# Memory denominators on GpSimd, a split last tile, four output buffers, an earlier load of x and a new order of work

## The chip, the cores and the metric

The kernel runs on one core of a Trainium2 chip. The time is device microseconds (us) for one execution of the whole program. The engines are TensorE (PE: matrix products), VectorE (DVE), ScalarE (ACT), GpSimd (POOL) and SyncE (SP, which here only issues transfers). They run side by side; each takes its own instructions strictly in the order in which the program lists them, and waits where one of them needs something that another engine or a transfer has not finished.

## What is computed

Two branches share one input x (2048 tokens, 512 features) and are mixed per token: `out = g * a + (1 - g) * b` with `g = sigmoid(x . gate_w)`.

Branch a is attention with a memory: 32 heads of 16 features, the tokens cut into 4 segments of 512. In each segment every head does causal softmax attention inside the segment, and reads a memory that the earlier segments have filled:

```python
p = softmax(q k^T * scale + mask);  a_dot = p v
pq = phi(q);  num = pq M;  den = pq z + 1e-06;  a_mem = num / den
o = sigmoid(beta) * a_mem + (1 - sigmoid(beta)) * a_dot
M = M + phi(k)^T v;  z = z + sum(phi(k))       # phi(t) = t + 1 for t > 0, else exp(t)
```

The outputs of the heads are multiplied by `wo`. Branch b is a gated feed-forward layer: `(gelu(x w_gate) * (x w_up)) w_down`, with 1792 hidden features. All tensors are bfloat16.

## The kernel before

**Tiling.** x is held transposed (`xT`: features on the 128 partitions, four chunks of features, 2048 tokens). A projection of 128 features for one segment is four matmuls of 512 columns; once the first logits have been made each is split into four column tiles that run at once (`mm4`). The pieces have short names with segment and index: `q`, `k`, `v` (projections), `gt` (two tiles of the gate projection), `up` (one tile), `lg` (a slot of logits of four heads, 20 slots a segment, numbered 0 to 79), `pv` (probabilities times values, for the even `e` or odd `o` heads of a chunk), `M` (memory update), `den` and `num` (memory denominators and numerators), `dn` and `wo` (one step of the down projection and of the output projection of 128 tokens, into the same accumulator).

**What follows each on other engines.** An `e` in front of a name is the evacuation of a PSUM result to SBUF (`eup2.9`, `epv0.3e`, `enum1.0`, `eden1`), by DVE or ACT. ACT does the exponentials of the logits (`ex20a`, `ex20b`) and the gelus (`egt`). GpSimd then zeroes the part of the exp tiles above the diagonal (`as20a`, `as20b`). `E`, `Q`, `Em`, `ph` make phi, the last on GpSimd. `ko` makes a copy of k for the odd heads. `r`, `rg`, `n`, `m`, `o` normalise the output of a chunk of eight heads, add the memory's part and transpose it into `xT`, where `wo` reads it. For the memory, `mbd` and `zbd` (DVE) lay M and z out by blocks; `eden` transposes the denominators, `rma` (`f_a`) spreads them over the partitions while adding 1e-06, `rmr` takes the reciprocal, `rmg` multiplies by the gate; then `nm` scales each `num`. `rma` is sixteen instructions of 32 partitions and 32 elements. `wos` scales `wo` once by the share of the direct attention. `os` scales a finished tile of 128 tokens into an output buffer `osb`, and `st` stores it.

**Buffers.** PSUM has two banks for most pieces (`gen`, a and b) and three double banks for logits and gate pairs (`lg`, a to c). A piece of TensorE cannot start before its bank's last content has been evacuated. In SBUF, rings of fixed size do the same (`RINGS`): twelve exp tiles `pT`, two `T` tiles of `pv`, one `rm`, one `Tm` (shared by `eden` and `enum`), two output buffers `osb`.

**The order is written out by hand.** `ORDER` lists every piece once; `Sched.run` emits them in that sequence, each to its engine. `#a` names the PSUM bank; `@A`, `@D`, `@P` choose ACT, DVE or POOL where a piece may run on several. So the order in the list is, engine by engine, the order in which each engine's queue is worked off.

**Loads.** All on SP's queue, in this order: the first half of `wk` and x of segment 0 (with ACT's queue), `wq`, the first 512 columns of `w_gate`, `wv`, the rest of `w_gate`, `w_up`, `gate_w`, `beta`, x of segments 1 to 3 (four transposing transfers each, `load_x`), `wo`. Then the transfers of `ORDER` follow (`pk`: transposing phi(k), `wdn`: the down weights, `st`: the stores).

**Around the change.** Between the logits of two segments (before `lg20`, `lg40`) TensorE does the seven gate pairs of a later segment, while ACT changes from exp to gelu and back; `den1` and `den2` fall there, and `den3` near `lg70`. In front of `lg0` it does the gate pairs of segments 0 and 1.

Of the kernel before, what the change touches and what calls it, by code (L numbers as in the profile page):

```python
# [49 lines left out]
lg16#ca ev1.1@D as14a v1.0#b ex16a up1.7#a ev1.0@D ex16b lg17#bc eup1.7 k1.2#b ex17a Emk1.0 r0.1  # L50
phk1.0 pv0.2o#a ek1.2@A lg18#ab ex17b epv0.2o v1.2#b ex18a k1.3#a ev1.2@D Eq1.0 lg19#ca ek1.3@D
q1.2#b ex18b r0.2 Emq1.0 up1.8#a Qq1.0 omz ex19a phq1.0 gt2.0#b eup1.8 o0.0 as17b M0.0#a rg0.1
Ek1.1 gt2.2#c pk1.0 as18a n0.1 eq1.2@A ex19b rg0.2 eM0.0 Emk1.1 up1.9#b eb egt2.0 as19b M0.1#a
gt2.3#a o0.1 Qk1.1 eM0.1 phk1.1 q1.3#a egt2.2 gt2.4#b eq1.3@A as18b Eq1.1 as15b as16b up1.13#a
as16a gt2.5#c as17a eup1.13 egt2.3 Qq1.1 zbd0 eup1.9 up1.10#a Emq1.1 n0.2 phq1.1 up1.11#b eup1.10
egt2.5 gt2.1#a eup1.11 mbd0 as19a den1#a egt2.1 gt2.6#c eden1 egt2.4 rma1 pv0.3e#b egt2.6 v1.3#a
epv0.3e lg20#ab ev1.3@D pv0.3o#b ex20a up1.12#a epv0.3o up2.0#b eup1.12 num1.0#a ex20b eup2.0
lg21#ca enum1.0 up2.1#b ex21a rmr1 up2.2#a ex21b as21a eup2.1 lg22#bc eup2.2 k2.0#b as21b ex22a
rmg1 k2.1#a nm1.0@P ek2.0@D ex22b lg23#ab ek2.1@D as20b num1.1#b ex23a as22a enum1.1 up2.3#a as22b
r0.3 ex23b as20a lg24#ca rg0.3 q2.0#b as23a eup2.3 ex24a nm1.1@P pv1.0e#a eq2.0@D Ek2.0 lg25#bc  # L60
ko1.2@P epv1.0e num1.2#b as24a ex24b enum1.2 up2.4#a as23b n0.3 ex25a as24b q2.1#b eup2.4 ex25b
lg26#ab nm1.2@D dn0.0.0#a Emk2.0 dn0.0.1 ex26a dn0.0.2 eq2.1@D dn0.0.3 dn0.0.4 ko1.1@D dn0.0.5
num1.3#b o0.3 ex26b lg27#ca dn0.0.6 enum1.3 dn0.0.7 ex27a dn0.0.8 as26b o0.2 dn0.0.9 dn0.0.10
pv1.0o#b wos ex27b as27a lg28#bc dn0.0.11 dn0.0.12 epv1.0o ex28a dn0.0.13 wo0.0.0 as26a wo0.0.1
wo0.0.2 wo0.0.3 ex28b as27b lg29#ab os0.0@D up2.6#b as25b ex29a as28a st0.0 as25a up2.5#a pk1.1
eup2.6 ex29b as29a lg30#ca eup2.5 pv1.1e#b ex30a as29b v2.0#a epv1.1e as28b ex30b r1.0 lg31#bc
ev2.0@D pv1.1o#b ex31a Qk2.0 v2.2#a ko1.3@D phk2.0 epv1.1o ex31b lg32#ab ev2.2@D v2.3#b rg1.0
ex32a dn0.1.0#a dn0.1.1 as31a ev2.3@D dn0.1.2 ex32b lg33#ca dn0.1.3 as30a n1.0 up2.7#b ex33a
dn0.1.4 eup2.7 dn0.1.5 ex33b dn0.1.6 lg34#bc m1.0@D v2.1#b ex34a as33b as32a dn0.1.7 ev2.1@D
dn0.1.8 dn0.1.9 ex34b ko2.0@P lg35#ab up2.8#b as30b ex35a as31b dn0.1.10 as32b eup2.8 dn0.1.11  # L70
dn0.1.12 lg36#ca as34b pv1.2e#b ex36a as35a dn0.1.13 as34a epv1.2e wo0.1.0 wo0.1.1 ex36b wo0.1.2
wo0.1.3 dn0.2.0#b dn0.2.1 dn0.2.2 os0.1@A dn0.2.3 lg37#ca st0.1 M1.0#a ex37a dn0.2.4 eM1.0 dn0.2.5
dn0.2.6 dn0.2.7 k2.2#a as37a as33a dn0.2.8 ek2.2@A dn0.2.9 dn0.2.10 dn0.2.11 ex37b dn0.2.12
dn0.2.13 pv1.2o#a Eq2.0 wo0.2.0 epv1.2o wo0.2.1 wo0.2.2 wo0.2.3 ex35b lg38#ca os0.2@D q2.2#a ex38a
Qq2.0 st0.2 dn0.3.0#b pk2.0 eq2.2@D dn0.3.1 dn0.3.2 dn0.3.3 r1.2 dn0.3.4 Emq2.0 dn0.3.5 dn0.3.6
r1.1 dn0.3.7 phq2.0 dn0.3.8 rg1.1 dn0.3.9 k2.3#a lg39#bc dn0.3.10 ex39a as36a dn0.3.11 ek2.3@D
dn0.3.12 dn0.3.13 ko2.1@P wo0.3.0 q2.3#a ex39b as37b wo0.3.1 as38a Ek2.1 eq2.3@D gt3.0#b as39a
as35b ex38b Qk2.1 Emk2.1 wo0.3.2 n1.1 phk2.1 egt3.0 gt3.4#c rg1.2 up2.10#a as36b Eq2.1 wo0.3.3
eup2.10 gt3.3#a as39b m1.1@D nm1.3@P os0.3@D M1.1#a gt3.1#b st0.3 egt3.3 eM1.1 as38b zbd1 mbd1
Qq2.1 pv1.3e#b Emq2.1 pv1.3o#a phq2.1 egt3.1 gt3.2#a epv1.3o egt3.4 o1.1 o1.0 gt3.5#b epv1.3e n1.2  # L80
r1.3 den2#a egt3.5 gt3.6#c eden2 egt3.2 rma2 up2.9#b egt3.6 lg40#ba eup2.9 up2.11#a ex40a up2.12#b
eup2.11 up3.0#a eup2.12 ex40b lg41#cb eup3.0 num2.0#b ex41a enum2.0 k3.0#a rmr2 up2.13#b ek3.0@A
rg1.3 rmg2 ex41b lg42#ac nm2.0@P eup2.13 up3.1#a ex42a n1.3 as41a up3.2#b eup3.1 ex42b lg43#ba
as40b eup3.2 num2.1#a as42a ex43a enum2.1 up3.3#b m1.2@D ex43b lg44#cb nm2.1@P eup3.3 k3.1#a ex44a
m1.3@D as43b q3.0#b ek3.1@D ex44b as42b lg45#ac eq3.0@D as40a num2.2#a ex45a as43a enum2.2 up3.4#b
# [934 lines left out]
```

## Time and profile before

| | us |
|---|---|
| median of 3 runs (lowest, highest) | 279.96 (279.3, 280.32) |
| profiled execution, whole | 279.55 |
| its span | 277.8 |
| TensorE busy | 266.5 (96%) |
| ACT busy | 218.4 (79%) |
| DVE busy | 178.2 (64%) |
| POOL busy | 151.6 (55%) |

The span runs from the first to the last instruction of the profiled execution. In the profile, PE is TensorE, PEld its weight loads, and SPq the queue of transfers that SP issues. L349 and the like are lines of the kernel; many pieces share the line of a helper, so they are told apart by the tile that they write (`dn`, `up`, `pv`). In a timeline a row is: start, duration, engine, line, operation, output<-input, shape, count; in square brackets stands how long the engine was idle ahead of it, and what it waited for. In a row of waits: who waited, for whom, us in total, times, longest. In a row of groups: busy us and mean ns behind the first bar, idle us behind the second. "PE busy" counts a matmul from its start to its modelled end, and they overlap.

### The profile page before, as it was taken

To read this page: it belongs to the slowest core of one execution; us is meant where nothing else is said; L and a number is where in the kernel's file an instruction comes from. 1 tells how busy PE (TensorE), PEld (TensorE's weight loads), DVE (VectorE), ACT (ScalarE), POOL (GpSimd) and SP (SyncE) were. 2 spreads that over 40 slices of the span, in tenths; PEclk is the share of its full clock that TensorE was granted. 3 is DMA by queue.
4 is the path that set the end of the run, shared out by engine and by line. 5 is a ranking of instruction groups with operands and counts; after the bars stand their busy time and mean duration, and the time that the engine had idled before them with its cause. 6 is when DMAs were issued, how large, how long until landed. Compare 5 with 4: busy or idle time off the path is not lost.

```text
span 277.8 us, 10843 instructions
## 1 busy us (share of the span) xinstructions
PE 266.5 (96%) x4855; PEld 129.0 (46%) x4855; DVE 178.2 (64%) x360; ACT 218.4 (79%) x234; POOL 151.6 (55%) x241
## 2 busy tenths in 40 slices
PE   7999999999999979999999998999999999899993
PEld 4644444444445544444454563444454454344541
DVE  1600026965878698997527688975947877956661
ACT  2388599999998985989875968989999898868400
POOL 8040004778846713954935940597597857349710
PEclk9999999999999999999999999999999999999999
DMA  6998492100002000003004000000002000100002
GB/s 207 371 286 107 95 310 67 33 12 2 4 2 42 2 0 2 2 2 59 2 24 61 2 21 2 2 2 22 2 5 59 2 22 2 40 22 21 21 2 79
DMA packets 22103, 14.07 MB, mean 51 GB/s; under 512 B 14120, under 2 KB 21032, under 8 KB 22056
## 3 DMA queue, kind: packets, MB, share of 16 engines
q1 hardware_dynamic: 21480, 12.85, 18.8%
q8 instruction: 38, 0.62, 1.0%
...
q14 instruction: 9, 0.07, 0.1%
HBM read 8.13 MB, written 2.10 MB: 37 GB/s over the span
## 4 chain that ended last, share of the span: by engine, by line
PE 78%; DVE 13%; DMA 6%; issue 1%; SPq 1%; ACT 0%; DVEq 0%; ACTq 0%
PE dn L349 19%; PE up L349 17%; PE lg L625 8%; PE gt L345 8%; PE gt L349 6%; PE pv L676 6%; PE v L349 4%; PE q L349 4%; DMA wga<-in_B_w_gate_dram 4%; PE k L349 4%; DVE rm L855 3%; DVE G L548 2%; DVE Mbd L816 1%; DMA out_dram<-osb 1%; DMA wdn<-in_A_x_dram 1%
## 5 line engine op out<-in xcount | busy, mean ns | idle before, releaser
L648 ACT ACTIVATE pT<-lg 128x1024 bf16<-128x1024 f32 x160 | 154.0, 1026 | 19.3 <-PE lg L625 18.1
L657 POOL TENSOR_SCALAR_AFFINE_SELECT pT<-pT 128x512 bf16<-128x512 bf16 (+1 forms) x160 | 88.5, 581 | 71.3 <-ACT pT L648 70.3
L349 PE MATMUL dn<-wdn,G 128*32 128x512 bf16 x896 | 59.3, 380 | 0.3 <-DVE T L694 0.3
L349 PE MATMUL up<-xT,wup 128*32 128x512 bf16 x896 | 56.1, 380 | 1.7 <-DVE G L548 1.2
L548 DVE TENSOR_TENSOR G<-up,G 128x512 bf16<-128x512 f32 x56 | 38.3, 688 | 19.0 <-PE up L349 15.5
L539 ACT ACTIVATE G<-gt 128x1024 bf16<-128x1024 f32 x28 | 27.4, 1022 | 9.3 <-PE gt L345 5.1
L349 PEld LDWEIGHTS <-wup 128*32 128x32 bf16 x896 | 23.3, 96 | 23.6 <-issue 5.8
L694 DVE STREAM_TRANSPOSE T<-pv 128x512 f32<-128x512 f32 x32 | 22.7, 710 | 17.5 <-PE pv L676 17.4
L349 PEld LDWEIGHTS <-G 128*32 128x32 bf16 x896 | 22.7, 96 | 21.5 <-issue 3.3
L211 DVE CAST vz<-v 128x512 bf16<-128x512 f32 x15 | 10.3, 689 | 28.9 <-PE v L345 25.3
L349 PE MATMUL gt<-xT,wga 128*32 128x512 bf16 x448 | 26.6, 379 | 0.0
L676 PE MATMUL pv<-pT,vz 128*32 128x256 bf16 (+2 forms) x640 | 23.1, 273 | 3.0 <-DVE T L694 1.7
L345 PE MATMUL gt<-xT,wga 128*128 128x512 bf16 x112 | 25.0, 379 | 0.1
L676 PEld LDWEIGHTS <-vz 128*32 128x32 bf16 x640 | 15.1, 97 | 12.4 <-issue 2.8
L751 POOL TENSOR_TENSOR pkT<-E,Q 128x1024 bf16<-128x1024 bf16 x6 | 12.8, 2128 | 13.4 <-DVE Q L744 6.4
L349 PE MATMUL dn<-wo,xT 128*32 128x512 bf16 x256 | 19.1, 380 | 0.0
L751 POOL TENSOR_TENSOR pq<-E,Q 128x1024 bf16<-128x1024 bf16 x6 | 13.2, 2194 | 10.6 <-DVE E L747 8.2
L349 PEld LDWEIGHTS <-wga 128*32 128x32 bf16 x448 | 12.9, 97 | 10.0
L625 PE MATMUL lg<-qT,kT 16*128 16x256 bf16 (+2 forms) x320 | 17.3, 274 | 0.0
L625 PE MATMUL lg<-qT,kO 32*128 32x128 bf16 (+2 forms) x320 | 17.3, 272 | 0.0
L345 PEld LDWEIGHTS <-wga 128*128 128x128 bf16 x112 | 10.8, 98 | 13.4 <-DMA wga<-in_B_w_gate_dram 0.6
L349 PEld LDWEIGHTS <-xT 128*32 128x32 bf16 x480 | 11.8, 96 | 11.0 <-issue 2.2
...
## 6 DMA issues: line engine op xcount, KB each, us to landing
...
wup<-in_B_w_up_dram SPq DMA_DIRECT2D x1, 1792.0 KB, 14.6
wdn<-in_B_w_down_dram SPq DMA_DIRECT2D x1, 1792.0 KB
...
```

Source lines behind the costliest of these rows:

```text
L211: nc.vector.tensor_copy(dst, src)
L345: nc.tensor.matmul(out, lhsT=lhsT, rhs=rhs, start=start, stop=stop)
L349: nc.tensor.matmul(out[a], lhsT=lhsT[:, a], rhs=rhs, start=start, stop=stop, tile_position=(0, 32 * j), skip_group_check=True)
L539: nc.scalar.activation(G[s][:, 2 * hp:2 * hp + 2, :], t[:, :, :], AF.Gelu_apprx_tanh)
L548: UPT[(s, hs)] = evac("DVE", g, box, lambda e, t: nc.vector.tensor_mul(G[s][:, hs, :], t[:, :], G[s][:, hs, :]), kind="up")
L625: nc.tensor.matmul(A[j // 2][:, j % 2, at * P:(at + nq) * P], lhsT=l, rhs=r, start=True, stop=True, tile_position=(32 * j, 0))
L648: nc.scalar.activation(pT[(s, t, h)][:, :, :], A[h][:, :, :], AF.Exp, scale=0.25)
L657: nc.gpsimd.affine_select(out=v, in_=v, pattern=pat, compare_op=ALU.is_ge, fill=0.0, base=0, channel_multiplier=-1)
L676: nc.tensor.matmul(t[32 * j:32 * j + 32, qb * P:(qb + nq) * P], lhsT=vz[s % 2][:, kt, h * VW:h * VW + 32], rhs=pT[(s, t0 + w, j // 2)][:, ...
L694: nc.vector.transpose(TT[key][:, e, :, :].rearrange("p a b -> p (a b)"), t[:, :])
L751: nc.gpsimd.tensor_add(d[:, :, :], box["E"][:, :, :], box["Q"][:, :, :])
L855: nc.vector.tensor_scalar_add(RMt[s][32 * j:32 * j + 32, c, :, :], bx["Td"][32 * c:32 * c + 32, :, 2 * j:2 * j + 2], 1e-6)
```

## The change

1. `rma1`, `rma2` and `rma3` go from DVE to GpSimd (`eng_of[e].tensor_scalar_add`, `@P` in the order).
2. The last tile of tokens (`os3.3`) is evacuated in two halves, columns 0 to 255 by DVE and 256 to 511 by ACT; the first half is stored from SP's queue and the second from ACT's.
3. Four output buffers `osb` in place of two.
4. The four transposing loads of x of segment 1 are issued ahead of `w_up`.
5. The order is another one throughout, and names the buffer of each exp tile (`#a` to `#l`). Some pieces change engine with it: `ko` is 8 times on DVE and 8 on GpSimd before, 13 and 3 after; `os` (whole tiles) 13 on DVE and 3 on ACT before, 9 and 6 after, and the two halves; two `ev` and two `eq` more are on ACT; `m` is on GpSimd 6 times in place of 4, `nm` 8 times in place of 9.

```diff
@@ ORDER, from lg0 back: the first gate pairs
-q0.0#b ek0.3@A ek0.1@D ek0.0@D q0.2#a eq0.0@D Ek0.0 gt0.0#b ... q0.3#b ... gt0.1#c ... gt0.4#a ... gt0.3#b
- ... gt0.6#c ... gt0.5#a gt0.2#b egt0.6 v0.2#a egt0.2 gt1.0#c gt1.5#b
+q0.2#a ek0.0@A ek0.1@D q0.3#b ko0.0@P Ek0.0 gt0.0#b ... gt0.1#c ek0.2@D egt0.0
+Emk0.0 ko0.1@D phk0.0 q0.0#b v0.2#a egt0.1 gt0.5#a Ek0.1 gt0.3#b egt0.5 gt1.4#c eq0.0@A gt1.0#a
@@ ORDER, around den1
-... mbd0 as19a den1#a egt2.1 gt2.6#c eden1 egt2.4 rma1 pv0.3e#b egt2.6 v1.3#a
-epv0.3e lg20#ab ev1.3@D pv0.3o#b ex20a up1.12#a epv0.3o up2.0#b eup1.12 num1.0#a ex20b eup2.0
-lg21#ca enum1.0 up2.1#b ex21a rmr1
+mbd0 den1#b egt2.5 gt2.6#b n0.2 egt2.2 eden1 pv0.3e#a rma1@P egt2.6 lg20#ca epv0.3e
+pv0.3o#b ex20a#k v1.3#a epv0.3o up1.12#b ev1.3@D up2.0#a eup1.12 ex20b#l as20a ko1.0@P lg21#bc
+eup2.0 up2.1#b ex21a#a rmr1 up2.2#a ex21b#b eup2.1 lg22#ab eup2.2 num1.0#b ex22a#g enum1.0
@@ ORDER, around den2
-... egt3.0 gt3.4#c rg1.2 up2.10#a as36b Eq2.1 ... egt3.3 eM1.1 as38b zbd1 mbd1 Qq2.1 pv1.3e#b Emq2.1
-pv1.3o#a phq2.1 egt3.1 gt3.2#a epv1.3o egt3.4 o1.1 o1.0 gt3.5#b epv1.3e n1.2
-r1.3 den2#a egt3.5 gt3.6#c eden2 egt3.2 rma2 up2.9#b egt3.6 lg40#ba
+... egt3.0 gt3.2#a eq2.3@D n1.2 gt3.5#c as37b egt3.2 pk2.1 n1.1 as39a gt3.3#b egt3.5 as39b Eq2.1 as38b
+wo0.3.0 m1.2@P wo0.3.1 wo0.3.2 pv1.3e#b wo0.3.3 gt3.1#a os0.3@A Qq2.1 epv1.3e egt3.3 st0.3 m1.1@D
+up2.10#a ko2.1@D zbd1 Emq2.1 o1.1 phq2.1 pv1.3o#b eup2.10 gt3.4#c egt3.1 o1.2 den2#a egt3.4
+gt3.6#b eden2 epv1.3o rma2@P r1.3 up2.9#a egt3.6 lg40#ac eup2.9 up2.11#b ex40a#i up2.12#a eup2.11
+up3.0#b eup2.12 ex40b#j as40a lg41#ba eup3.0 num2.0#a ex41a#a rg1.3 enum2.0 k3.0#b as40b rmr2
+up2.13#a ek3.0@A n1.3 ex41b#b lg42#cb rmg2 up3.1#b eup2.13 nm2.0@P ex42a#k up3.2#a
@@ ORDER, around den3
+pv3.0e#b ex65b#l as63a lg66#ab epv3.0e dn1.3.12 ex66a#a dn1.3.13 mbd2 wo1.3.0 up3.13#b ex66b#b as66a
+lg67#ca eup3.13 wo1.3.1 as65b ex67a#g wo1.3.2 Emq3.1 as66b wo1.3.3 dn2.0.0#b os1.3@D
+... den3#a dn2.0.13 eden3 wo2.0.0 as69a lg70#ca wo2.0.1 rg3.0 ex70a#f rma3@P wo2.0.2
+... wo2.0.3 lg71#cb os2.0@D dn2.1.9 as70a ex71a#a dn2.1.10 as69b ko3.3@D dn2.1.11 st2.0 num3.0#b
+dn2.1.12 as70b dn2.1.13 ex71b#b enum3.0 lg72#ac as68a wo2.1.0 n3.0 wo2.1.1 ex72a#k wo2.1.2 as71b
+dn2.2.0#b rmr3 wo2.1.3 dn2.2.1 dn2.2.2 as68b dn2.2.3 os2.1@D lg73#ba as72a dn2.2.4 ex73a#l rmg3
+dn2.2.5 pv3.1o#a nm3.0@P
@@ ORDER, the end
-wo3.1.3 dn3.3.7 os3.1@D ... dn3.3.8 os3.2@D dn3.3.9 st3.1 ... st3.2 dn3.3.13 wo3.3.0 wo3.3.1
-wo3.0.0 wo3.3.2 wo3.3.3 wo3.0.1 os3.3@D wo3.0.2 wo3.0.3 os3.0@A st3.3 st3.0
+pv3.3o#b dn3.3.4 epv3.3o dn3.3.5 dn3.3.6 dn3.2.9 o3.2 dn3.1.6 dn3.3.7 dn3.2.10 r3.3 dn3.2.11 dn3.2.12
+rg3.3 dn3.2.13 n3.3 wo3.2.0 dn3.3.8 wo3.0.1 m3.3@D dn3.3.9 dn3.1.7 wo3.0.2 o3.3 dn3.3.10 wo3.2.1
+wo3.2.2 wo3.0.3 dn3.1.8 os3.0@A wo3.2.3 dn3.1.9 os3.2@D dn3.3.11 dn3.1.10 st3.0 dn3.1.11 dn3.1.12
+st3.2 dn3.3.12 dn3.3.13 dn3.1.13 wo3.1.0 wo3.1.1 wo3.3.0 wo3.1.2 wo3.1.3 wo3.3.1 os3.1@A wo3.3.2
+wo3.3.3 os3.3.256 os3.3.0 st3.1 st3.3.256 st3.3.0
@@
-        self.pools = ("lg", "gen")
+        self.pools = ("lg", "gen", "pT")
@@
-             "osb": 2, "G": 3}
+             "osb": 4, "G": 3}
@@
     nc.sync.dma_start(wga[:, :, 4 * P:DFF], wgr[:, :, 4 * P:DFF])
+    load_x(1)
     load_w(nc.sync, wup, B_w_up)
...
-    for s in range(1, NSEG):
+    for s in range(2, NSEG):
         load_x(s)
@@
-        def f_a(_):
+        def f_a(e):
...
-                    nc.vector.tensor_scalar_add(
+                    eng_of[e].tensor_scalar_add(
...
-        a = add(f"rma{s}", "DVE", f_a, ...
+        a = add(f"rma{s}", ["POOL", "DVE"], f_a, ...
@@ out_group
+        split = (s, qt) == (NSEG - 1, KT - 1)
...
+        halves = [(0, D // 2), (D // 2, D)] if split else [(0, D)]
...
+        for n, (lo, hi) in zip(("DVE", "ACT"), halves):
+            ev = add(f"os{s}.{qt}.{lo}", n, lambda e, lo=lo, hi=hi: fn(e, lo, hi), kind="osh",
+                     deps=[g, TAB["omz"]], frees=[(ring, first)])
+            q = nc.scalar if n == "ACT" else nc.sync
+            add(f"st{s}.{qt}.{lo}", "ACT" if n == "ACT" else "SP",
+                lambda _, q=q, lo=lo, hi=hi: store(q, s, qt, bx["o"], lo, hi), kind="st",
+                deps=[ev], frees=[("osb", g)])
```

The two halves of the last tile become `os3.3.0` (DVE, columns from 0) and `os3.3.256` (ACT).

More of the change, by code (lines that the diff above doesn't have):

```diff
@@ L50 @@
[L50 to L85, printed above, removed]
```

198 lines of the change are left out of this document (123 added, 75 removed).

## The prediction

> **What bounds the kernel now.** I read the page's busy shares first, then the engines' busy time by stretch, then the waits of TensorE, then the timelines around the waits. All times are us from the start of the span.
>
> ```profile
> PE 266.5 (96%) x4855; PEld 129.0 (46%) x4855; DVE 178.2 (64%) x360; ACT 218.4 (79%) x234; POOL 151.6 (55%) x241
> ```
>
> ```profile
> 0.00:15.90 15.90, 14.17 (x82) 7.88 (x82) 6.02 (x15) 6.04 (x9) 8.46 (x18) 1.00 0.88 304
> 15.90:38.70 22.80, 22.77 (x106) 10.09 (x107) 0.00 (x0) 17.62 (x20) 1.44 (x1) 1.00 0.91 162
> 38.70:98.00 59.30, 59.30 (x1209) 28.68 (x1211) 43.19 (x84) 54.41 (x60) 38.63 (x78) 1.00 0.14 37
> 98.00:106.00 8.00, 6.30 (x132) 3.64 (x126) 7.25 (x25) 6.18 (x6) 0.61 (x1) 1.00 0.01 2
> 106.00:165.90 59.90, 59.17 (x1216) 28.96 (x1215) 43.67 (x79) 49.15 (x51) 38.60 (x50) 1.00 0.11 20
> 165.90:172.00 6.10, 5.40 (x97) 2.60 (x93) 4.89 (x20) 5.83 (x6) 0.00 (x0) 1.00 0.01 3
> 172.00:236.00 64.00, 63.15 (x1320) 29.84 (x1313) 47.90 (x86) 58.91 (x64) 44.82 (x68) 1.00 0.05 13
> 236.00:244.00 8.00, 6.67 (x140) 3.06 (x132) 7.06 (x24) 6.26 (x7) 3.34 (x7) 1.00 0.11 35
> 244.00:273.60 29.60, 29.60 (x588) 14.30 (x580) 17.52 (x31) 13.34 (x14) 15.71 (x22) 1.00 0.07 22
> 273.60:277.80 4.20, 0.01 (x2) 0.00 (x0) 0.75 (x1) 0.69 (x1) 0.00 (x0) 1.00 0.26 87
> ```
>
> Columns: stretch, its length, busy PE, weight loads, DVE, ACT, POOL, granted clock, DMA share, GB/s. TensorE is full from 15.90 to 273.60 at clock 1.00, but for three short stretches, 98 to 106 (1.70 idle), 165.9 to 172 (0.70) and 236 to 244 (1.33), and smaller gaps of 0.73 and 0.85 in the long ones beside them; then 4.20 follow in which it does nothing. The change gives TensorE the same 4855 matmuls, so it can win only those idle pieces, in all 1.70 + 0.70 + 1.33 + 0.73 + 0.85 = 5.3, a part of the 4.20, and little of the first 15.90 (1.73 idle, mostly before the first data). What it can lose is any new wait in a queue that is full.
>
> ```profile
> PE pv L676 <- DVE T L694: 1.7, 1, 1.7
> PE pv L676 <- DVE Tm L882: 1.3, 1, 1.3
> PE up L349 <- DVE G L548: 1.2, 3, 0.7
> ```
>
> Each large wait of TensorE is for an evacuation on DVE. The DVE timeline at the first one:
>
> ```profile
> 97.11 2.05 DVE L816 TENSOR_TENSOR Mbd<-Macc,bdeb 128x128 bf16<-128x128 f32 x4
> 99.09 0.70 DVE L849 STREAM_TRANSPOSE Tm<-den 128x512 f32<-128x512 f32 x1
> 99.82 2.96 DVE L855 TENSOR_SCALAR rm<-Tm 32x32 f32<-32x32 f32 x16
> 102.81 0.72 DVE L694 STREAM_TRANSPOSE T<-pv 128x512 f32<-128x512 f32 x1
> ```
>
> The sixteen small additions of `rma1` (2.96) stand on DVE ahead of the evacuation of `pv0.3e`, and TensorE's next `pv` needs that evacuation's bank. The same piece is the cause at the second and third stretch:
>
> ```profile
> 237.41 3.62 DVE L855 TENSOR_SCALAR rm<-Tm 32x32 f32<-32x32 f32 x16
> ```
>
> **The sum is made against the profiled execution**, 279.55 (span 277.8 and 1.75 around it). The median of the runs is 279.96, so 0.4 is added at the end.
>
> **1. `rma` from DVE to GpSimd.** It leaves DVE 2.96 to 3.62 shorter three times. What it costs GpSimd is bounded by its own small copies and its own scalar operation:
>
> ```profile
> L509 POOL COPY G<-Tm 32x16 f32<-32x16 f32 x16 | 3.1, 196 | 0.7
> L378 POOL TENSOR_SCALAR kO<-kT,odd 128x512 bf16<-128x512 bf16 x8 | 12.5, 1562 | 0.0
> ```
>
> Sixteen at 0.196 are 3.1; at the other end sixteen at 1.56 would be 25. The additions have 32 elements a partition like the copies' 16, and 480 fewer than `kO`, so I take 0.20, 3.2 per `rma`. First place, new order: on DVE behind `eden1` stand `epv0.3e`, `epv0.3o`, `ev1.3`, `eup1.12`, `eup2.0`, then `rmr1`: five evacuations at about 0.7 are 3.5, more than the 3.2 of GpSimd, so `rmr1` does not wait. On TensorE, `gt2.6`, `pv0.3e` and `lg20` follow `den1` and `v1.3` is now behind `pv0.3o`. With before's times `eden1` ends at 99.8 (about 0.8 later in the new order, where `n0.2` stands ahead of it) and TensorE gets to `pv0.3o` at 101; its bank is free. The 1.70 goes: **-1.7**. Behind it, GpSimd has `as20a`, `ko1.0` and `nm1.0`; `pv1.0e` needs the selects behind those, about at the time it is reached, as before: 0. If that cover is gone, the queue's delay is added to `pv1.0e` one for one.
>
> Second place. The wait for `eup2.9` and those behind it goes:
>
> ```profile
> 170.91 1.46 PE L349 MATMUL up<-xT,wup 128*32 128x512 bf16 x21 [0.70 <-DVE G L548]
> ...
> 165.91 0.40 PE L839 MATMUL den<-pq,zbd 128*32 128x512 bf16 x4
> ```
>
> ```profile
> 162.16 2.13 POOL L751 TENSOR_TENSOR pq<-E,Q 128x1024 bf16<-128x1024 bf16 x1 [1.50 <-DVE E L747]
> ```
>
> But `phq2.1` ends at 164.29, 1.6 ahead of `den2`, and in the new order it starts later: `Eq2.1` on ACT stands behind three gelus in place of one, and `Emq2.1` on DVE behind `epv1.3e`, `m1.1` and `ko2.1` as well. I count 2 to 2.3 of delay, so `den2` waits about 0.5, and with DVE pressed behind it (`rmr2`, `n1.3` and `rmg2` now stand in a row ahead of `eup2.13`, at 0.9 + 0.8 + 0.3) some 0.4 more at `up3.2`. -0.7 + 0.9 = **+0.2** (ends -0.7 and +1.5, the latter nearly the largest wait seen, 1.7).
>
> Third place. In the new order `rmr3` comes after `os2.0`, `ko3.3`, `enum3.0` and `n3.0`; the 1.33 at `pv3.1o` goes. But DVE takes `mbd2` (2.05 in the row above) ahead of `eup3.13`, whose bank `dn2.0.0` wants: about 0.6; and `os2.1` now holds `pv3.1o` for about 0.3. -1.3 + 0.9 = **-0.4** (ends -1.3 and +0.6).
>
> **2. The port that DVE and GpSimd share.** One row shows what stands against moving work to GpSimd:
>
> ```profile
> 149.03 1.97 DVE L707 TENSOR_TENSOR r<-r,G 128x32 f32<-128x32 f32 x1
> ```
>
> ```profile
> 148.82 2.12 POOL L751 TENSOR_TENSOR pq<-E,Q 128x1024 bf16<-128x1024 bf16 x1 [5.25 <-DVE E L747]
> ```
>
> A tiny product of DVE took 1.97 and ended as GpSimd's addition ended. An `rma` instruction on GpSimd lasts 0.2, so a DVE operation of that kind loses 0.2 at a time; in the windows of `rma` DVE does mostly evacuations from PSUM. I take 0 (ends 0 and +0.6: one such loss at each of three places). The Trainium skill (SBUF — State Buffer, section "SBUF: two separate sides") says that the pair of ports is an exclusive lock for the whole instruction, against a DVE operation with two SBUF inputs or in a 2-port mode, and the row agrees. By that rule the five `ko` that move from GpSimd to DVE would be exposed too, and the sum would be up to 0.6 higher.
>
> **3. `wos` earlier.** The four scalings of `wo` (2.43) stood just ahead of the first use:
>
> ```profile
> 121.31 2.43 DVE L571 TENSOR_SCALAR wo<-wo,omg 128x512 bf16<-128x512 bf16 x4
> ```
>
> ```profile
> 122.75 1.45 PE L349 MATMUL dn<-wo,xT 128*32 128x512 bf16 x16
> ...
> 169.16 1.05 PE L349 MATMUL up<-xT,wup 128*32 128x512 bf16 x16
> ```
>
> Sixteen matmuls of this form take 1.05 where nothing holds them (the second row), here 1.45. In the new order `wos` runs beside segment 0's last steps, where TensorE has the gate groups: **-0.4** (ends -0.4 and 0).
>
> **4. x of segment 1 ahead of the up weights.** On SP's queue:
>
> ```profile
> 5.13 0.80 SPq L288 DMA_DIRECT2D wga<-in_B_w_gate_dram  x1
> 6.01 1.02 SPq L272 DMA_DIRECT2D wup<-in_B_w_up_dram  x1
> ...
> 12.65 19.88 SPq L267 DMA_TRANSPOSE xT<-in_A_x_dram  x12
> ```
>
> ```profile
> wup<-in_B_w_up_dram SPq DMA_DIRECT2D x1, 1792.0 KB, 14.6
> ```
>
> ```profile
> L349 PE MATMUL up<-xT,wup x228: 379/379/392, 42.2 to 59.8; 128*32 128x512 bf16 x114
> ```
>
> ```profile
> 5.13 10.76 DMA wga<-in_B_w_gate_dram
> ```
>
> ```profile
> DMA to landing us min/median/max: 2.7/2.9/10.3
> ```
>
> (The last is of the tile `xT`.) Four of the twelve issues, a third of 19.88 or 6.6, now precede `wup`, `gw` and `beta`; these start about 6.6 later, x1 as much earlier, everything behind is where it was. `wup` would land near 21 + 7 = 28 (it took 14.6 from issue), its first use stays at 42.2: free, with 14 to spare. x1 is now wanted at about 20 by `gt1.4`, the fifth gate pair in place of the eighth. The issues end near 12.6 and queue behind the gate weights (landed at 5.13 + 10.76 = 15.9); the median landing is 2.9 behind an issue, the worst of the twelve 10.3. Taking the gate weights' end plus about 3, x1 is there at 19: 0, ends 0 and +3. The opening order also puts `ext0.0` behind `ext2.0` (one half evacuation, an estimate of 0.4 from the 0.7 of whole ones), against a wait for the gate weights that `v0.2` now fills: **+0.1**.
>
> **5. The tail.**
>
> ```profile
> 271.71 1.90 PE L349 MATMUL dn<-wo,xT 128*32 128x512 bf16 x32
> 273.90 0.75 DVE L945 TENSOR_SCALAR osb<-dn,omz 128x512 bf16<-128x512 f32 x1 [2.50 <-DMA out_dram<-osb]
> 274.44 0.69 ACT L943 ACTIVATE osb<-dn,omz 128x512 bf16<-128x512 f32 x1 [14.53 <-DMA out_dram<-osb]
> ```
>
> With two output buffers `os3.3` and `os3.0` wait for stores; the last evacuation ends at 275.13, 1.5 behind TensorE's end at 273.61, and 2.7 pass from it to the end of the span. With four buffers none waits. The new last steps: `wo3.1.3`, then three more `wo` (about 0.22 each, by 1.90 for eight); `os3.1` on ACT (0.69) starts some 0.3 ahead of TensorE's end, and the half tile of `os3.3` behind it ends about 0.4 + 0.4 = 0.8 past that end at the latest (a half, taken at 0.4 of a whole 0.69 to 0.75). Then the store, 2.7 as before: 1.5 - 0.6 = 0.9, **-0.9** (ends -1.2 and 0, if two stores on SP and one on ACT meet). The 2.9 between 271.4 and 274.3 in the chain is not saved whole, because TensorE is busy until 273.6 anyway.
>
> **6. The rest of the order.** In the last 12 the order puts the chain `pv3.3o`, `o3.2`, `n3.3`, `m3.3`, `o3.3` just ahead of `wo3.0.3`, and `pv3.3e` behind GpSimd's `as76b`: **+0.3** (ends 0 and +1). Going through the other lists with these durations I found no wait longer than 0.3, but where before has gaps of 0.73 and 0.85 in 124 the new order will have its own: **+0.4** beyond these (ends -0.8 and +2). Five `ko` move from GpSimd to DVE, two `ev`, two `eq` and three whole `os` from DVE to ACT, two `m` to GpSimd and one `nm` from it: engines at 55 to 79%, behind a TensorE that is full, so 0; where one is the last evacuation ahead of a bank it costs its own 0.4 to 0.7.
>
> ```profile
> ACT pT L648 <- POOL pT L657: 0.4, 2, 0.2
> ```
>
> The exp tiles keep twelve buffers, now named in the order; ACT waits only 0.4 in all for GpSimd over them, so I take 0 (ends -0.4 and +0.4).
>
> Sum: -1.7 + 0.2 - 0.4 - 0.4 + 0.1 - 0.9 + 0.3 + 0.4 = -2.4; 279.55 - 2.4 = 277.15, and with the 0.4 to the median about 277.5.
>
> **Rivals.** *A. No net gain.* The order trades each evacuation wait for another; the terms of 1 and 6 then sum to 0 and only 3 to 5 remain, and these shrink by small waits: 279 to 281. For it: the second place above, where I find as much new as old. Against: the largest wait, 1.70, has nothing in its place. *B. GpSimd becomes late (slower).* Place: `rmr1`, which needs `rma1` 3.5 behind `eden1`. Each 0.1 over 0.22 per addition puts 1.6 on each of three places. At 0.4 it is 3 x 2.9 = 8.7, less 2 of slack: some +4 against the forecast's gain, 282; it decides from about 0.30, where 3 x 1.3 eats 2.4. For it: `kO`'s 1.56; against: the copies' 0.196. *C. x1 late.* TensorE stands at `gt1.4` up to 3: 280.5. *D. All old waits vanish and none comes:* 279.96 - 5.3 - 0.9 = 273.8.
>
> **How the numbers follow.** Forecast (275.5 to 278.5) 0.49; D 0.07; A 0.25; C 0.08; B 0.11. Half a per cent, 1.4, is about what a measurement of this kernel can tell from no change: faster is below 278.56, same up to 281.36. The forecast and D are 0.56 faster; A (but 0.01) and half of C 0.28 same; B, half of C and that 0.01 are 0.16 slower. The range that leaves out two in ten reaches from D's side to the end of C: 274.3 to 281.5; the forecast's own is 275.5 to 278.5.
>
> **What would show it.** Right: `rma` on POOL at 3 to 3.5 each, PE idle under 0.6 from 98 to 106, no `osb` wait on a store, the last evacuation under 0.9 behind TensorE's end, `wo0.0` matmuls at 1.05. Wrong: `den2` or `up3.2` without a wait; `rmr` waiting for POOL; PE idle at the first gate pairs of segment 1; new waits for `as` in front of `pv`. The forecast fails if the small waits that I did not find add up to over 2.

## The result, and the profile after

Before 279.69 us (median of 14 runs, 278.67 to 281.92), after 276.57 us: ratio 0.9891, 95% interval [0.9866, 0.9917]. The predicted time was 277.5. The profiled execution of the changed kernel has a span of 275.2, against 277.8.

The busy shares of the changed kernel:

```profile
PE 266.5 (97%) x4855; PEld 130.5 (47%) x4855; DVE 163.5 (59%) x309; ACT 222.7 (81%) x242; POOL 156.5 (57%) x285
```

TensorE has the same 4855 matmuls and the same 266.5. DVE lost 14.7 us, and it was not the bound. So the gain has to be idle time of TensorE. The changed kernel by stretch (length, then busy PE, weight loads, DVE, ACT, POOL, granted clock, DMA share, GB/s):

```profile
39.10:98.00 58.90, 58.90 (x1201) 28.41 (x1204) 42.94 (x83) 54.30 (x60) 37.80 (x78) 1.00 0.11 26
98.00:106.00 8.00, 8.00 (x168) 4.81 (x164) 5.96 (x11) 6.85 (x7) 4.98 (x17) 1.00 0.01 2
106.00:165.00 59.00, 57.90 (x1196) 29.01 (x1192) 40.37 (x78) 51.42 (x56) 36.27 (x50) 1.00 0.11 25
165.00:172.00 7.00, 6.87 (x128) 3.16 (x124) 4.98 (x9) 5.92 (x6) 5.17 (x18) 1.00 0.01 2
172.00:236.00 64.00, 63.65 (x1328) 29.93 (x1324) 44.12 (x82) 59.36 (x66) 41.84 (x69) 1.00 0.04 11
236.00:244.00 8.00, 6.93 (x136) 3.23 (x132) 4.58 (x8) 5.51 (x7) 7.30 (x19) 1.00 0.06 18
271.30:275.20 3.90, 0.00 (x0) 0.00 (x0) 0.48 (x1) 0.56 (x2) 0.00 (x0) 1.00 0.22 69
```

Length minus busy PE is the idle time. There is none from 39.10 to 98, and none from 244 to TensorE's end at 271.29. The five stretches from 98 to 244 had 1.70 + 0.73 + 0.70 + 0.85 + 1.33 = 5.3 before, and have 0 + 1.10 + 0.13 + 0.35 + 1.07 = 2.65 now: 2.7 won. The tail in which TensorE does nothing went from 4.2 to 3.9: 0.3 won. The first logits, which began at 38.70, begin here at 39.15: 0.45 lost. 2.7 + 0.3 - 0.45 is 2.5, and the spans differ by 2.6.

The larger waits of TensorE that are left, behind one of 1.2 at the very start that both kernels have (total, times, longest):

```profile
PE k L350 <- DVE xT L215: 0.9, 2, 0.6
PE dn L354 <- DVE Tm L887: 0.9, 1, 0.9
PE lg L630 <- POOL kO L383: 0.8, 1, 0.8
```

The first is in the opening, before the first logits. The other two are new, and both come from one number: what `rma` takes on GpSimd. GpSimd's own timeline at the first and third place, and the group of all 48 additions (busy us, mean ns):

```profile
100.54 5.48 POOL L860 TENSOR_SCALAR rm<-Tm 32x32 f32<-32x32 f32 x16 [2.08 <-DVE Tm L854]
106.09 0.41 POOL L662 TENSOR_SCALAR_AFFINE_SELECT pT<-pT 128x256 bf16<-128x256 bf16 x1
106.49 1.56 POOL L383 TENSOR_SCALAR kO<-kT,odd 128x512 bf16<-128x512 bf16 x1
...
234.18 5.55 POOL L860 TENSOR_SCALAR rm<-Tm 32x32 f32<-32x32 f32 x16 [0.19 <-DVE r L712]
```

```profile
L860 POOL TENSOR_SCALAR rm<-Tm 32x32 f32<-32x32 f32 x48 | 13.7, 285 | 7.2 <-DVE Tm L854 4.2 <-DVE r L712 0.2
```

One addition lasts 0.285, and from one start to the next pass about 5.48 / 16 = 0.342, not 0.20. `rma` takes 5.5 and not 3.2. TensorE at the two places:

```profile
108.11 0.29 PE L630 MATMUL lg<-qT,kO 32*128 32x256 bf16 x4 [0.81 <-POOL kO L383]
...
240.53 0.40 PE L354 MATMUL dn<-wdn,G 128*32 128x512 bf16 x4 [0.92 <-DVE Tm L887]
```

At the first place `ko1.0` stands behind `rma1` in GpSimd's queue, ends at 108.05, and `lg22`, which reads it, starts at 108.11. At the third place DVE's `enum3.0` wants the single `Tm` tile that `rma3` still reads:

```profile
239.76 0.72 DVE L887 STREAM_TRANSPOSE Tm<-num 128x512 f32<-128x512 f32 x1 [1.91 <-POOL rm L860]
```

It waits 1.91 for GpSimd, and `dn2.2.0`, which needs the PSUM bank that `enum3.0` evacuates, waits 0.92.

### The profile page after: what moved, and what is told of

The parts are those of the page before. It is cut to its first block, busy times and chain, and to the rows that moved or that the text cites. A ratio compares the mean times of both kernels' runs of the same rounds, so it can differ in the third digit from the quotient of the medians.

```text
span 275.2 us, 10836 instructions
## 1 busy us (share of the span) xinstructions
PE 266.5 (97%) x4855; PEld 130.5 (47%) x4855; DVE 163.5 (59%) x309; ACT 222.7 (81%) x242; POOL 156.5 (57%) x285
## 4 chain that ended last, share of the span: by engine, by line
PE 88%; DVE 5%; POOL 4%; issue 1%; ACT 0%; POOLq 0%; DVEq 0%
PE dn L354 21%; PE up L354 17%; PE gt L350 9%; PE lg L630 8%; PE gt L354 8%; PE pv L681 6%; PE v L354 4%; PE k L354 4%; PE q L354 4%; POOL rm L860 3%; PE k L350 2%; DVE G L553 1%; PE warm L350 1%; PE q L350 1%; PE v L350 1%
## 5 line engine op out<-in xcount | busy, mean ns | idle before, releaser
L662 POOL TENSOR_SCALAR_AFFINE_SELECT pT<-pT 128x512 bf16<-128x512 bf16 (+1 forms) x160 | 86.8, 572 | 63.2 <-ACT pT L653 62.8
L354 PE MATMUL dn<-wdn,G 128*32 128x512 bf16 x896 | 61.4, 380 | 0.9 <-DVE Tm L887 0.9
L215 DVE CAST vz<-v 128x512 bf16<-128x512 f32 x13 | 9.0, 689 | 30.2 <-PE v L350 24.2
L354 PE MATMUL dn<-wo,xT 128*32 128x512 bf16 x256 | 19.7, 380 | 0.0
L354 PEld LDWEIGHTS <-wga 128*32 128x32 bf16 x448 | 13.8, 97 | 9.6
L860 POOL TENSOR_SCALAR rm<-Tm 32x32 f32<-32x32 f32 x48 | 13.7, 285 | 7.2 <-DVE Tm L854 4.2
```

Source lines behind the costliest of these rows:

```text
L215: nc.vector.tensor_copy(dst, src)
L354: nc.tensor.matmul(out[a], lhsT=lhsT[:, a], rhs=rhs, start=start, stop=stop, tile_position=(0, 32 * j), skip_group_check=True)
L662: nc.gpsimd.affine_select(out=v, in_=v, pattern=pat, compare_op=ALU.is_ge, fill=0.0, base=0, channel_multiplier=-1)
L860: eng_of[e].tensor_scalar_add(RMt[s][32 * j:32 * j + 32, c, :, :], bx["Td"][32 * c:32 * c + 32, :, 2 * j:2 * j + 2], 1e-6)
```

## The experiments

The theory: the gain is idle time of TensorE, and it takes both the move of `rma` and the order that keeps other pieces out of its way; what is left of the waits is the price of 0.342 per addition. The rivals: the move alone did it; the order alone did it; or buffers, x or the split tile did. Ratios are to the kernel before, measured beside each kernel.

| kernel | ratio | 95% interval | span of its profile |
|---|---|---|---|
| after | 0.9891 | 0.9866 to 0.9917 | 275.2 |
| after again | 0.9875 | 0.9846 to 0.9903 | 274.6 |
| after, `rma` back on DVE | 0.9981 | 0.9956 to 1.0007 | 277.7 |
| before, `rma` on GpSimd only | 1.0036 | 1.0016 to 1.0056 | 278.8 |
| after, x of segment 1 back behind `w_up` | 0.9997 | 0.9960 to 1.0033 | 280.5 |
| after, two output buffers | 0.9921 | 0.9885 to 0.9956 | 275.3 |
| before, four output buffers only | 0.9961 | 0.9946 to 0.9976 | 277.7 |
| after, last tile whole | 0.9876 | 0.9837 to 0.9914 | 275.4 |
| after, `ko1.0` and `rma3` on DVE | 0.9898 | 0.9872 to 0.9923 | 274.2 |
| the same, with the opening of before | 0.9865 | 0.9838 to 0.9891 | 275.8 |
| after, `rma` as copies | 0.9829 | 0.9800 to 0.9857 | 273.7 |
| the same, four more edits | 0.9800 | 0.9777 to 0.9823 | 273.3 |

### The move of `rma`, undone and alone

After, with `rma` on DVE:

```diff
-rma1@P ... rma2@P ... rma3@P
+rma1@D ... rma2@D ... rma3@D
```

> The changed kernel with rma1, rma2 and rma3 back on VectorE, in the same places of the order; nothing else. Theory: the move to GpSimd is worth something at the first two places although sixteen additions take 5.5 us there, and costs at the third. By the changed kernel's trace: place 1, eden1 ends at 100.45, plus 2.96 on VectorE, so the evacuation of pv0.3e ends near 104.1 in place of 101.94 and v1.3 waits 2.1; the 1.0 that lg22 and num1.0 lose for ko1.0 behind rma1 goes: +1.1. Place 2: epv1.3o ends near 169.4 and up2.11 waits 1.6: +1.6. Place 3: enum3.0 comes earlier, dn2.2.0's wait of 1.09 shrinks to 0.3: -0.8. Sum +1.9 on 276.6: about 278.5 us. Rival 1, GpSimd's slowness gives back all that VectorE wins: 276.6 within 0.5. Rival 2, the move carries the whole gain: about 279.6.

Nearly all of the gain is lost, more than expected: 0.9981. TensorE's larger waits in this kernel:

```profile
PE v L354 <- DVE T L699: 2.1, 1, 2.1
PE up L354 <- DVE G L553: 1.3, 1, 1.3
...
PE num L354 <- DVE osb L959: 1.0, 1, 1.0
```

They stand at the three places of `rma`. The third had been expected to shrink to 0.3 with `rma3` on DVE, yet the 3.90 that it takes there holds back `os2.0` and with it `num3.0`. From 98 to 244 this profile has 5.3 of idle time of TensorE again, as much as before. So all the rest of the change without the move (the order, the buffers, the load of x and the split) is worth next to nothing.

Before, with the move alone:

```diff
-        def f_a(_):
+        def f_a(e):
...
-                    nc.vector.tensor_scalar_add(
+                    eng_of[e].tensor_scalar_add(
...
-        a = add(f"rma{s}", "DVE", f_a, ...
+        a = add(f"rma{s}", "POOL", f_a, ...
```

> The kernel before with rma1, rma2 and rma3 on GpSimd, in its own old order; nothing else. Theory: the move pays at the first two places and costs at the third, where enum3.0 and what stands behind it wait for sixteen additions of 5.5 us in place of 3.6: the waits of 1.8 at pv0.3o and 0.9 at up2.12 go, the one at pv3.1o grows by about 1.5: -1.1, near 278.6 us, ratio 0.996; in the trace GpSimd's rma lasts 5.4 to 5.6. Rival: without the new order GpSimd's queue turns it into a loss at each place, over 280.5. Other rival: the move alone is the whole gain, 276.6, ratio 0.989.

A miss: not a gain but 1.0036. Nine of its twelve runs have a mean granted clock of 0.986 to 0.994 and took 280.6 to 282.3; the three at 1.00 took 278.6, 280.3 and 280.5, where before had 280.06 beside them. The profile is of one of these three, so where the others lost their clock is not shown, and what the move loses apart from the clock is not told apart from nothing. The kernel's largest wait of TensorE, and `rma3` on GpSimd:

```profile
PE pv L676 <- DVE Tm L882: 3.3, 1, 3.3
```

```profile
236.02 5.50 POOL L855 TENSOR_SCALAR rm<-Tm 32x32 f32<-32x32 f32 x16
```

The waits of 1.7 and 0.7 at the first two places go, but in the old order `rmr3`, `enum3.0` and `epv3.1o` follow `rma3` at once, and the wait at `pv3.1o` grows from 1.3 to 3.3. This is rival B's mechanism, on the slower engine's price, at one place of three. Some 2.1 are won at two places and 2.0 lost at the third; that this span is 1.0 longer all the same (TensorE ends 0.6 later, the tail is 0.4 longer) has no single wait behind it. The move alone gives nothing, and the rest without it next to nothing. Together they give the larger part of the gain: without the four buffers the changed kernel still has 0.9921 (below).

### x of segment 1

```diff
-    load_x(1)
     load_w(nc.sync, wup, B_w_up)
...
-    for s in range(2, NSEG):
+    for s in range(1, NSEG):
```

> The changed kernel with the four loads of x of segment 1 back behind the up weights, gate_w and beta; the order stays. Theory: the load's place is needed by the new order. x of segment 1 was there at 24.5 in the kernel before, gt1.4 now starts at 20.72: TensorE waits 3 to 4 there, and the time is 279.5 to 280.6 us. Rival: the up weights leave room on the queues and the transposes land as early: 276.6.

Most of the gain is gone: 0.9997, with runs from 278.1 to 282.3. TensorE's timeline between 16 and 32 in the profile, which is of the 282.3:

```profile
16.77 3.62 PE L349 MATMUL gt<-xT,wga 128*128 128x512 bf16 x16
23.06 2.20 PE L349 MATMUL gt<-xT,wga 128*128 128x512 bf16 x4 [2.68 <-DMA xT<-in_A_x_dram]
25.48 6.84 PE L349 MATMUL gt<-xT,wga 128*128 128x512 bf16 x22 [0.22 <-issue]
```

and its stretches (columns as above; the granted clock is third from the end):

```profile
16.80:20.40 3.60, 3.58 (x17) 1.44 (x15) 0.00 (x0) 3.56 (x4) 0.00 (x0) 1.00 1.29 261
20.40:23.06 2.66, 0.00 (x0) 0.00 (x0) 0.00 (x0) 2.46 (x4) 0.00 (x0) 0.90 1.41 105
23.06:25.30 2.24, 2.05 (x4) 0.69 (x6) 0.00 (x0) 0.00 (x0) 0.00 (x0) 0.50 0.68 136
25.30:29.40 4.10, 3.92 (x10) 1.44 (x10) 0.00 (x0) 0.00 (x0) 0.00 (x0) 0.50 0.50 112
29.40:34.00 4.60, 4.60 (x23) 2.11 (x22) 0.00 (x0) 3.42 (x4) 0.00 (x0) 1.00 0.50 91
```

Two things are seen. `gt1.4` waits 2.7 for x. Within this wait the granted clock falls to 0.50 (0.90 is the mean of its 2.66, so by an estimate for the last 0.5 of it); it stays there for the next 6.3 us, and the matmuls come 0.427 apart instead of 0.216; that costs about half of 6.3, some 3.1 more. 2.7 + 3.1 = 5.8 is about the 5.6 by which the first logits come later in this profile (44.77 against 39.15). The clock is not lost in every run: the five that took 281.5 to 282.3 have a mean granted clock of 0.988 to 0.994, the seven that took 278.1 to 279.5 one of 0.997 to 1.00. The median of the seven, 279.2, lies 1.0 below the 280.18 of before beside them, and 2.6 above after's 276.57, about the wait alone. Of the five only one was profiled; that the others lost their clock at the same wait is likely, not shown. Before has 0.03 of idle time between 15.90 and 38.70, so there the load ahead of `w_up` could hardly win anything; that was not run. It is what the new order of the gate groups, with `gt1.4` in fifth place, needs in order not to lose.

The Trainium skill (TensorE: Matmul & The Clock Gate, section "Part 1: The HAM clock gate (the "warmup" mystery)") says that an idle TensorE is throttled to half its clock and that at least one window of about 3.4 us of work releases it. The half clock agrees with the 0.50, and the 6.3 until it came back do not contradict the release. For the cause the section counts at least one idle window of about 3.4, while here a wait of 2.66 was enough. The measurement decides for this kernel.

### Output buffers and the split tile

After, with two output buffers:

```diff
-             "osb": 4, "G": 3}
+             "osb": 2, "G": 3}
```

> The changed kernel with two output buffers in place of four. Theory: in the new order the last evacuations are further apart, so only the two halves of the last tile wait, for the store of os3.2 (issued near 268.7, landed near 271.7, while they start at 271.3 to 271.9): +0.2 to +0.5, 276.8 to 277.1 us. Rival, as the prediction had it, the four buffers carry the gain at the tail: +0.9 or more, 277.5.

The evacuation of `os3.1` on ACT has to wait for a store again:

```profile
ACT osb L957 <- DMA out_dram<-osb: 3.8, 1, 3.8
```

Not all of the 3.8 is the store's: in after the same evacuation starts 0.59 ahead of TensorE's end, and here it starts at 270.89, which is about 1.2 later than that. TensorE ends at 270.23 in this profile and the span at 275.3, so the tail is 5.1 against 3.9. The intervals of 0.9921 and 0.9891 overlap, so in time the 1.2 is not told apart from less.

Before, with four:

```diff
-             "osb": 2, "G": 3}
+             "osb": 4, "G": 3}
```

> The kernel before with four output buffers, nothing else. Theory: os3.3 no longer waits for a store and os3.0 follows TensorE's end at once, so the last evacuation ends 0.8 behind TensorE's end in place of 1.5: -0.7, about 279.0 us, ratio 0.9975. Rival: the order around the stores gives it back (nothing under 0.3), or the stores' own time on the queue is what sets the end.

0.9961, the one part that is a gain by itself. The last evacuation starts right behind TensorE's end (274.30):

```profile
274.36 0.69 ACT L943 ACTIVATE osb<-dn,omz 128x512 bf16<-128x512 f32 x1 [13.74 <-PE dn L349]
```

The tail is 3.4 against 4.2, without any split.

After, with the last tile whole on DVE:

```diff
-wo3.3.3 os3.3.256 os3.3.0 st3.1 st3.3.256 st3.3.0
+wo3.3.3 os3.3@D st3.1 st3.3
...
-        split = (s, qt) == (NSEG - 1, KT - 1)
+        split = False
```

> The changed kernel with the last tile evacuated whole by VectorE and stored by one transfer from SP. Theory: the split brings nothing, because the half on VectorE waits for the half on ScalarE (it started at 271.91, as ScalarE's ended): a whole evacuation would run from about 271.5 to 272.25, where the second half ends at 272.39 now; 276.5 us, within 0.3 of the changed kernel. Rival: halves end earlier and their two stores overlap, so without them it is 0.5 to 0.9 longer: 277.1 to 277.5.

0.9876: not told apart from after, so the split is worth nothing that can be measured. The reason stands in the tail of the changed kernel:

```profile
269.39 1.90 PE L354 MATMUL dn<-wo,xT 128*32 128x512 bf16 x32
...
270.70 1.17 ACT L957 ACTIVATE osb<-dn,omz 128x512 bf16<-128x512 f32 x2 [2.55 <-PE dn L354]
271.90 0.35 ACTq L912 DMA_DIRECT2D out_dram<-osb  x1
271.91 0.48 DVE L959 TENSOR_SCALAR osb<-dn,omz 128x256 bf16<-128x256 f32 x1 [3.26 <-ACT osb L957]
```

TensorE ends at 271.29. The half on DVE could start there, but starts at 271.91, when ACT's half has ended: the halves run one behind the other. Whether they are held apart by the shared output tile or by the shared accumulator was tested by giving each half a tile of its own:

```diff
-                bx["o"] = rtile("osb", [P, D])
+                for lo in (0, D // 2):
+                    bx[lo] = rp.tile([P, D // 2], BF, name="osh", tag=f"osh{lo}", bufs=1)
```

> The changed kernel with a buffer of its own for each half of the last tile. Theory: the half on VectorE waits for the one on ScalarE because both read the same accumulator, so it still starts as that ends, 0.6 behind TensorE's end. Rival: they are kept apart only because they write one buffer: then it starts 0.1 to 0.2 behind TensorE's end and the span is 0.4 shorter. Prediction's view, that neither waits, is the same as the rival.

```profile
270.91 0.47 ACT L959 ACTIVATE osh<-dn,omz 128x256 bf16<-128x256 f32 x1
...
271.41 0.48 DVE L961 TENSOR_SCALAR osh<-dn,omz 128x256 bf16<-128x256 f32 x1 [3.21 <-ACT osh L959]
```

DVE's half still starts only as ACT's ends (270.91 + 0.47). Its one run took 276.52. So it is not the output tile that holds them apart, which leaves the accumulator as the likely cause; no run separates that from anything else the halves share. The Trainium skill (PSUM — Partial Sum Buffer, section "PSUM bank collisions raise a hardware error") says that two engines may not touch the same partitions of a bank at once, readers included, and that software must order them; the trace agrees with such an order. Whether halves in two banks would gain was not tried.

### What the price of `rma` still costs

If GpSimd's queue behind `rma1` and the `Tm` tile behind `rma3` make the two new waits, taking `ko1.0` and `rma3` to DVE should take them away:

```diff
-ko1.0@P ... rma3@P
+ko1.0@D ... rma3@D
```

> The changed kernel with ko1.0 and rma3 on VectorE; nothing else. Theory: the two largest waits left in it, 1.0 at lg22 and num1.0 (ko1.0 stands behind rma1 on GpSimd) and 1.1 at dn2.2.0 (enum3.0 waits for rma3), are the price of 5.5 us of additions in GpSimd's queue; both go, os2.0 starts 0.3 later: TensorE's end comes 1.5 to 2.0 earlier, 274.6 to 275.1 us, ratio 0.982 to 0.984. Rival: the waits move to the next piece that VectorE is late with, and the time stays within 0.5 of 276.6.

A miss: 0.9898, no better than after. Its six runs fall apart, two at 275.5 and 275.9 and four from 277.1 to 277.8. The profile is of the 275.9, with a span 1.0 shorter than after's, so what the four lost is not shown. In the profile the wait at `dn2.2.0` goes, but another comes a few pieces earlier:

```profile
PE num L354 <- DVE osb L959: 1.0, 1, 1.0
```

```profile
233.75 3.90 DVE L860 TENSOR_SCALAR rm<-Tm 32x32 f32<-32x32 f32 x16
237.69 0.75 DVE L959 TENSOR_SCALAR osb<-dn,omz 128x512 bf16<-128x512 f32 x1
```

`rma3` holds `os2.0` back on DVE, and `num3.0` waits for its bank. At this place the move of `rma3` is about even: 1.0 on DVE, 0.9 on GpSimd. With `ko1.0` on DVE the 0.81 at `lg22` goes, and 0.3 and 0.2 come at `num1.0` and the `k` behind it.

The same kernel with the opening of before, where the gate pairs and x stay as after:

```diff
-... xt2.0 xt3.0 ext1.0 ext2.0 ext0.0 k0f0.0 k0f1.0 xt0.1 ... ext2.1 ext3.1 k0f0.1 ext3.0 k0f1.1 ...
+... xt2.0 ext0.0 xt3.0 ext1.0 k0f0.0 xt0.1 ... k0f1.0 ext2.0 ext3.1 k0f0.1 ext2.1 ext3.0 k0f1.1 ...
```

> As c_queue, and with the opening of the kernel before (the order of the eight half evacuations of x and the first matmuls of k). Theory: the new opening delays the first k by 0.5, which nothing hides because TensorE is full from there on: another -0.4 to -0.5, first logits near 38.7 in place of 39.16, about 274.3 us, ratio 0.981. Rival: TensorE then only waits longer for the gate weights at gt0.5, so nothing is gained.

0.9865, short of the gain expected, and not told apart from the kernel without the old opening. Its profile, which is of the longest of six runs (277.52, the median is 275.88), has a wait that the others lack:

```profile
91.80 2.13 POOL L756 TENSOR_TENSOR pkT<-E,Q 128x1024 bf16<-128x1024 bf16 x1 [6.08 <-DMA pk<-pkT]
```

In after the same row has

```profile
90.08 2.13 POOL L756 TENSOR_TENSOR pkT<-E,Q 128x1024 bf16<-128x1024 bf16 x1 [3.89 <-DMA pk<-pkT]
```

There is one `pkT` tile, `phk1.1` needs it back from the transposing transfer of `pk1.0`, and it came free 1.7 later here, though the transfer was issued 0.5 earlier (at 85.07, in after at 85.55). TensorE then waits for the gelus and for `pq` (1.0 and 0.7) ahead of `den1`. The after kernel itself was run again beside the next two:

> The changed kernel itself, as the measure for the runs beside it. Theory and rival alike: 276.6 us where the kernel before has 279.7, ratio 0.989.

0.9875. Between it and the first measurement lies 0.0016, which is the ground on which the small differences here stand.

The price itself was then attacked. Sixteen plain copies spread the denominators, and one DVE instruction over the whole tile adds 1e-06 ahead of the reciprocal; the computation is the same:

```diff
-                    eng_of[e].tensor_scalar_add(
+                    eng_of[e].tensor_copy(
                         ...
-                        bx["Td"][32 * c:32 * c + 32, :, 2 * j:2 * j + 2], 1e-6)
+                        bx["Td"][32 * c:32 * c + 32, :, 2 * j:2 * j + 2])
...
+            nc.vector.tensor_scalar_add(RMt[s][:, :, :, :], RMt[s][:, :, :, :], 1e-6)
```

> The changed kernel with the sixteen additions of each rma as plain copies on GpSimd, and the 1e-06 added by one VectorE instruction over the whole tile ahead of the reciprocal. Theory: GpSimd's scalar addition is what is dear (0.34 from one to the next), a copy of the same shape costs what the copies of the gate rows did (0.18 to 0.20): rma 3.0 to 3.3 in place of 5.5; the waits of 1.0 at lg22 and num1.0 and 1.1 at dn2.2.0 go, VectorE has 0.2 more three times: -1.5 to -2.0, 274.6 to 275.1 us. Rival: each instruction of GpSimd that moves 32 partitions costs the same, whatever it does: rma stays over 5 and the time at 276.6.

0.9829, against 0.9875 for after in the same series; the intervals overlap by 0.0011. The group and the first `rma` on GpSimd:

```profile
L860 POOL COPY rm<-Tm 32x32 f32<-32x32 f32 x48 | 9.9, 206 | 6.2 <-DVE Tm L854 4.2 <-DVE r L712 0.2
```

```profile
100.64 3.88 POOL L860 COPY rm<-Tm 32x32 f32<-32x32 f32 x16 [2.05 <-DVE Tm L854]
```

One copy takes 0.206, start to start 0.243: 3.9 per `rma`, a little over the expected 3.0 to 3.3. The waits at `lg22` and `dn2.2.0` are no longer among TensorE's waits, which shows the price of the scalar addition to be their cause.

Last, copies with four more edits: before's opening, `ko1.0` on DVE, two `pkT` tiles, and three output buffers (for room).

```diff
-             "pkT": 1, ...  "osb": 4, "G": 3}
+             "pkT": 2, ...  "osb": 3, "G": 3}
...
-ko1.0@P
+ko1.0@D
```

> As a_copy, with the opening of the kernel before, ko1.0 on VectorE, two buffers pkT in place of one (phk1.1 no longer waits for the transposing store pk1.0) and three output buffers in place of four, to make room. Theory: over a_copy the opening gives 0.4 to 0.5, and den1 no longer hangs on when the last part of a transfer lands: 274.0 to 274.6 us, ratio 0.980 to 0.982. Rival: TensorE has no more waits that these remove, and the time is that of a_copy.

0.9800, 274.97 us, faster than both kernels. Against the copies alone the intervals overlap, so the four edits together are probably, but not surely, worth something, and none of them was measured by itself. The places that had waits:

```profile
106.00:165.00 59.00, 58.51 (x1209) 29.29 (x1204) 40.85 (x80) 52.14 (x56) 34.82 (x47) 1.00 0.11 25
...
236.00:244.00 8.00, 7.84 (x160) 3.46 (x160) 6.11 (x10) 6.39 (x8) 7.49 (x16) 1.00 0.07 20
```

Idle are 0.49 and 0.16, against 1.10 and 1.07 in after.

## Why the prediction was right, step by step

The sum came out (-2.4 forecast, about -2.5 by the stretches), but not from the terms as they were written: they were off by between -1.2 and +0.8, and that these errors cancel is luck. What was right is the mechanism, that the gain is idle time of TensorE which the move and the order take together.

| step | forecast | in the two profiles |
|---|---|---|
| first place | -1.7 | 1.70 gone, 0.81 new at `lg22`: -0.9 |
| second place | +0.2 | 0.70 to 0.13: -0.6 |
| third place | -0.4 | 1.33 to 1.07: -0.3 |
| `wos` earlier | -0.4 | the stretch 106 to 165 without `lg22`'s wait: 0.73 to 0.29, -0.4 |
| rest of the order, and its end | +0.4, +0.3 | 172 to 236: 0.85 to 0.35, -0.5; none at the end, 0 |
| opening | +0.1 | +0.45 (-0.23 in a second profile of after) |
| tail | -0.9 | -0.3 |

**What held.** TensorE is the bound, and only its idle time could be won. The wait at `pv0.3o` vanished (98 to 106 has no idle time). x was there in time for `gt1.4`. No store held an `osb`. `wo0.0` ran without the gaps.

**The price of `rma` was mis-sized**, 0.20 per addition against 0.342 measured. The nearest row was the copy's 0.196, and that is what sixteen copies nearly cost (0.206 each); but a scalar addition is another operation, and a mean duration is not the distance from start to start. Two steps failed with it: at the first place the forecast had 0 for the pieces behind `rma1` on GpSimd, and the delay came out there, at `ko1.0`, not at `rmr1`, which waited 0.41 and held up nobody; at the third the wait of 0.6 foreseen at `dn2.0.0` did not come, the one at `pv3.1o` was 0.15 and not 0.3, and 0.92 came at `dn2.2.0`, where none was foreseen.

**Rival B's condition was met** (it was to decide from 0.30) and the kernel was not slower. Its price, one for one at three places, gives 3 x 16 x (0.342 - 0.22) = 5.9, less 2 of slack, and was wrong: DVE, freed of `rma`, waits for TensorE between the evacuations (0.77, 0.29, 0.30 and 0.17 between 100.4 and 105), so `rmr1` was not wanted as early as the durations alone say. Only 0.81 + 0.92 of new waits reached TensorE. In the old order the same price took back at the third place what the other two had won.

**The second place was too pessimistic.** I counted 2 to 2.3 of delay for `phq2.1` and a wait of 0.5 at `den2`. GpSimd finished in time:

```profile
161.56 2.14 POOL L756 TENSOR_TENSOR pq<-E,Q 128x1024 bf16<-128x1024 bf16 x1 [2.25 <-DVE E L752]
...
164.57 0.40 PE L844 MATMUL den<-pq,zbd 128*32 128x512 bf16 x4
```

(The first row is GpSimd's timeline, the second TensorE's.) `pq` ended at 163.70, 0.87 ahead of `den2`. A later place in a queue had been taken for a later start; the engines in question were waiting, not full. A `den2` without a wait was one of the prediction's own signs of being wrong, and so was an `rmr` that waits for GpSimd; both were seen.

**The shared port** was taken at 0, and no new wait of TensorE comes from it. Its mark is there all the same. On DVE and on GpSimd in the changed kernel:

```profile
153.96 2.61 DVE L717 TENSOR_TENSOR N<-T,r 128x512 bf16<-128x512 f32 x2
```

```profile
152.84 2.14 POOL L756 TENSOR_TENSOR pkT<-E,Q 128x1024 bf16<-128x1024 bf16 x1 [2.35 <-DVE Q L749]
```

Two products that otherwise take about 0.7 each took 2.61, and end past the addition's end at 154.98. No wait of TensorE is listed behind them.

**The tail was over-priced.** The forecast had the last evacuation end at most 0.8 behind TensorE, and its sum took 0.6 without saying why. It ended at 272.39, 1.1 behind, since the halves do not overlap, and 2.8 passed from there to the end. What is won here comes with the four buffers, not with the split.

**The opening took 0.45 where 0.1 was forecast, but this is not shown to be the order's.** In this profile the first `k` begins at 5.47 (before: 4.93) after waiting 0.63 for an `ext`, and `q` at 10.36 (before: 9.59):

```profile
5.47 1.53 PE L350 MATMUL k<-xT,wk 128*128 128x256 bf16 x8 [0.63 <-DVE xT L215]
...
10.36 1.89 PE L350 MATMUL q<-xT,wq 128*128 128x512 bf16 x8
```

In the second profile of the same kernel (after again) the `ext` is waited for as well, yet `q` and the first logits come earlier:

```profile
5.28 1.03 PE L350 MATMUL k<-xT,wk 128*128 128x256 bf16 x8 [0.73 <-DVE xT L215]
...
9.67 1.89 PE L350 MATMUL q<-xT,wq 128*128 128x512 bf16 x8
```

There the first logits begin at 38.47, 0.23 earlier than before. Over all the profiles they begin at 38.62 to 39.38 with before's opening (five kernels) and at 38.47 to 39.31 with the new one (eight profiles, without the kernel that waits for x). So the two openings are not told apart, and the 0.45 is the spread of one execution.
